# One 8 KB load of a decode kernel taken as five loads of 1, 2, 4, 8 and 113 rows

## The chip, the core and the metric

The kernel runs on one core of a Trainium2 chip. A core has TensorE (PE, matrix multiplies; PEld is its weight load), VectorE (DVE), ScalarE (ACT), GpSimd (POOL) and SyncE (SP, which here only issues transfers), an on-chip memory of 128 partitions (SBUF), an accumulator memory for matmul results (PSUM), and 16 DMA engines that bring data in from HBM. The metric is the device time of one execution in microseconds; less is better.

## What is computed

Two layers, each of attention with a cached K and V (one new token for each of 4 sequences) and a gated feed-forward block, all in float32:

```python
B, Sq, D = 4, 1, 512
Hq, Hkv, Sk, Dh = 32, 8, 4096, 128
def _A_ref(x, k_cache, v_cache, wq, wo):
    q = (x @ wq).reshape(B, Sq, Hq, Dh).transpose(0, 2, 1, 3)
    k = jnp.repeat(k_cache, rep, axis=1)
    v = jnp.repeat(v_cache, rep, axis=1)
    scores = jnp.einsum("bhqd,bhkd->bhqk", q, k) * (Dh ** -0.5)
    p = _softmax(scores, axis=-1)
    o = jnp.einsum("bhqk,bhkd->bhqd", p, v)
    return o.transpose(0, 2, 1, 3).reshape(B, Sq, Hq * Dh) @ wo
def _B_ref(x, w1, w3, w2):          # F = 1792
    h = _silu(x @ w1) * (x @ w3)
    return h @ w2
x = A_x
x = x + _A_ref(_layernorm(x), ...)
x = x + _B_ref(_layernorm(x), ...)
x = x + _A_ref(_layernorm(x), ...)
x = x + _B_ref(_layernorm(x), ...)
```

Both layers use the same caches and weights. K and V together are 128 MB a layer, more than fits on the chip, so most of it is read twice.

## The kernel before

**Data.** The host lays all weights and caches out as one array `rows` of 128 rows; row p is what partition p is to hold. Its columns are counted in units of KB = 256 floats, that is 1 KB a partition and 128 KB over all partitions. In this order stand the projection weights, the caches group by group (a group is one of the 8 KV heads with its 4 query heads, REP = 4), and the feed-forward weights. A group has 32 tiles of 4 units: tiles 0 to 15 are its keys (two chunks of 2048 positions, 8 tiles each), 16 to 31 its values in the same order. In those units the keys of group 1 are 192 to 255 and its values 256 to 319; the keys of group 2 are 320 to 383 and its values 384 to 447, of which the last two tiles are 440 to 447.

**Space and loads.** SBUF holds one tensor `space` of 216 units a partition and, behind them, x. `LOADS` (lines 52 to 66) lists by hand every load in the order in which it is issued, as (first unit in `rows`, units, place in `space`); two entries marked "stash" are copies by ScalarE and no loads. `pump` (line 119) runs when the program is written out: whenever a tile has been used for the last time, `done` (line 148) marks its place free and calls `pump`, which issues as many entries of the list as have their place free, in order, on SP's queue. So a load's place in SP's queue is fixed, and on the chip its issue waits until what was read from its place before has been read. Each load is one `dma_start` at line 139 of all 128 rows (line 136 for the first, which brings x along).

**Compute.** Layer 0 goes through the groups 0 to 7, layer 1 through 7 to 0, so that most of group 7 can stay on the chip from one layer to the next. For each group: `score` (line 322, matmuls at line 333) multiplies q with the keys, `maximum` and `exponent` take the softmax's parts chunk by chunk, `turn` transposes the probabilities, and `weigh` (line 389, matmuls at line 395) multiplies them with the values. The second chunk's weighing stands in `finish`, and DVE adds up its results there (line 416). On PE the order is that of the program: the second weighing of a group stands ahead of the first scores of the next. TensorE takes a tile straight from `space`. Each of these matmuls shows as two in the trace: 32 for a chunk of scores or of weighing, 4 for a tile.

**Around the change,** in layer 1, the list reads (0, 32, 96), (384, 56, 128), (440, 8, 104), (192, 64, 28), (256, 64, 136), (32, 28, 29), (60, 36, 57), (96, 32, 120), and so on to the last values of group 0 and what is left of w3 and w2. (384, 56) are the values of group 2 but for the last two tiles, 7 MB; (440, 8) are those two, 8 KB a row, 1 MB; (192, 64) and (256, 64) are keys and values of group 1, 8 MB each. The keys go to the places 28 to 91. The values go to 136 to 199, on top of values of group 2 from (384, 56), so they wait for most of that group's weighing, but not for its last two tiles. (32, 28), the first keys of group 0, go to 29 to 56, where keys of group 1 lie.

Of the kernel before, what the change touches and what calls it, by code (L numbers as in the profile page):

```python
# [16 lines left out]
P = 128  # L17
# [25 lines left out]
KB = 256  # L43
# [22 lines left out]
)  # L66
BUSY = (4, 1, 2)
SCRATCH = 64

# [5 lines left out]
def tile_decode_layers(ctx: ExitStack, tc: tile.TileContext, rows, out):  # L75
    nc = tc.nc
# [9 lines left out]
    def place(at, n):  # L86
        return space[:, at * KB:(at + n) * KB]
# [31 lines left out]
    def pump():  # L119
        while state["next"] < len(LOADS):  # L120
            src, n, at = LOADS[state["next"]]
            if src == "stash":
                i, n = n, U // KB
                keys = [("kv", TURN, i)]
                if i == 0 and not state["back"]:
                    return
            else:
                keys = [key for key in stream if src <= offset[key] < src + n]
            if any(taken[at:at + n]):
                return  # L130
            taken[at:at + n] = [True] * n
            if src == "stash":
                for j in range(2):
                    nc.scalar.activation(place(at, n)[:, j * BLOCK:(j + 1) * BLOCK], stored[2 * i + j], AF.Copy)
            elif state["next"] == 0:
                nc.sync.dma_start(space[:, at * KB:], rows[:, 0:n * KB + P])
            else:
                lo = src * KB + (P if src else 0)
                nc.sync.dma_start(place(at, n), rows[:, lo:lo + n * KB])
            for key in keys:  # L140
                where[key] = at
                at += size[key[0]]
            state["next"] += 1
# [4 lines left out]
    def done(layer, *key):  # L148
        if layer == 0 and (key[0][:2] == "w1" or key[0] in ("wq", "wo") and key[1] >= HELD or key[:2] == ("kv", TURN) and key[2] in KEPT):
            return  # L150
        at, n = where[key], size[key[0]]
        taken[at:at + n] = [False] * n
        pump()

    pump()


# [47 lines left out]
    def busy(n):  # L205
        if n:
            pt = scores().rearrange("p (k c) -> p k c", k=KC)
            nc.tensor.matmul(pt[:, 0:n, :], ident, ident.unsqueeze(1).to_broadcast([P, n, P]),  # L208
                             start=True, stop=True)

    def small(name, bufs=1):
        return work.tile([P, 1], F32, name=name, tag=name, bufs=bufs)
# [30 lines left out]
    def layernorm(rowsum):  # L243
        xc = deviation(rowsum)
        xT = lay_down(xc)
        ssq = squares(xc)
        rstd = work.tile([P, 2], F32, name="rstd", bufs=1)

        def factor():
            var = o_ps[1][:, 1:2]  # L250
            mean(var, ssq)
            inverse(rstd[:, 0:1], var)

        return xT, rstd, factor
# [170 lines left out]
    def turn_o(o):  # L425
        nc.tensor.matmul(misc[:, 0:B * REP], o, head, start=True, stop=True)  # L426
        nc.vector.tensor_copy(oT[:, :, 0:B], misc[:, 0:B * REP].rearrange("p (b h) -> p h b", b=B))  # L427
# [5 lines left out]
    def project_o(layer, g, rowsum):  # L433
        w = wo_of(g)
        for h in range(REP):
            for k in range(KC):
                nc.tensor.matmul(x_ps[32 * k:32 * k + B, :], oT[:, h, 0:B], w[:, h, k * P:(k + 1) * P],
                                 start=(h == 0), stop=(h == REP - 1))
        done(layer, "wo", g)
        nc.vector.scalar_tensor_tensor(x_sb, x_ps, 1.0, x_sb, op0=ALU.mult, op1=ALU.add,  # L440
                                       accum_out=rowsum)
# [99 lines left out]
    for layer in range(LAYERS):  # L541
# [14 lines left out]
        for n, (g, (first, last)) in enumerate(order):  # L556
# [7 lines left out]
            if layer and n == 0:  # L564
                state["back"] = True
                pump()
# [22 lines left out]
        nc.scalar.activation(spare, half[:, 0:1], AF.Sigmoid)  # L589
        busy(BUSY[0])  # L590
        turn_o(o)
        busy(BUSY[1])
        rowsum = small("rowsum")
        project_o(layer, g, rowsum)
        busy(BUSY[2])
        xT, rstd, factor = layernorm(rowsum)
# [50 lines left out]
```

## Time and profile before

| | us |
|---|---|
| median of 3 runs | 704.23 |
| lowest, highest | 703.98, 705.48 |
| the profiled execution, its own time | 705.11 |
| its span, first to last instruction | 703.2 |
| PE busy in it | 420.1 (60%) |
| DVE busy | 145.8 (21%) |
| mean granted TensorE clock | 0.828 |

The profile shows one execution. Its page gives for each engine the busy time, then the span in 40 equal slices (each digit a share in tenths; here a slice is 17.6 us), the DMA packets and queues, and the chain of work that ended last: from the last instruction back, at each step to what released it. Other views of the same trace are used too: that chain in order of time (start, duration, what), the timeline of instructions (start, duration, engine and line, what is written from what, count, and in brackets the idle time before and what ended it), stretches of time with the busy time of each engine, the granted clock, the DMA engines' share and GB/s, and the DMA issues of a stretch with their size and the time from issue to landing. "SPq" is SP's queue, which issues transfers; "space<-in_rows" is a load.

### The profile page before, as it was taken

To read this page: it belongs to the slowest core of one execution; us is meant where nothing else is said; L and a number is where in the kernel's file an instruction comes from. 1 tells how busy PE (TensorE), PEld (TensorE's weight loads), DVE (VectorE), ACT (ScalarE), POOL (GpSimd) and SP (SyncE) were. 2 spreads that over 40 slices of the span, in tenths; PEclk is the share of its full clock that TensorE was granted. 3 is DMA by queue.
4 is the path that set the end of the run, shared out by engine and by line. 5 is a ranking of instruction groups with operands and counts; after the bars stand their busy time and mean duration, and the time that the engine had idled before them with its cause. 6 is when DMAs were issued, how large, how long until landed. Compare 5 with 4: busy or idle time off the path is not lost.

```text
span 703.2 us, 7344 instructions
## 1 busy us (share of the span) xinstructions
PE 420.1 (60%) x3218; PEld 135.7 (19%) x3218; DVE 145.8 (21%) x508; ACT 41.8 (6%) x100; POOL 3.1 (0%) x10
## 2 busy tenths in 40 slices
PE   1265466644767609767676994734554735557687
PEld 0111121201212103121233331201111201112125
DVE  3012111121121203331221242102120301202232
ACT  0010000000001000000201200100100001000010
POOL 0000000000000000000000000000000000000000
PEclk9997777776698858886998998867977968769899
DMA  9999999999999999999999999999999999999996
GB/s 417 421 418 433 455 418 417 448 440 426 435 427 429 435 429 422 431 431 425 420 403 409 416 433 434 448 425 424 449 430 412 450 418 434 447 426 426 420 419 271
DMA packets 12703, 298.39 MB, mean 424 GB/s; under 512 B 1408, under 2 KB 1536, under 8 KB 4352
## 3 DMA queue, kind: packets, MB, share of 16 engines
q1 hardware_dynamic: 12672, 297.93, 99.0%
q8 instruction: 25, 0.41, 0.2%
q14 instruction: 6, 0.05, 0.0%
HBM read 297.86 MB, written 0.07 MB: 424 GB/s over the span
## 4 chain that ended last, share of the span: by engine, by line
DMA 68%; PE 28%; DVE 2%; another core or an unknown queue 1%; issue 1%; ACT 1%; SPq 0%; ACTq 0%; DVEq 0%
DMA space<-in_rows 68%; PE o L395 10%; PE scores L333 10%; PE turned L359 1%; PE o L469 1%; PE sums_ps L317 1%; PE sums_ps L507 1%; ACT p L352 1%; PE scores L208 1%; PE stored L260 1%; DVE acc L346 1%; PE stored L447 0%; DVE pT L361 0%; PE sums_ps L306 0%
## 5 line engine op out<-in xcount | busy, mean ns | idle before, releaser
L333 PE MATMUL scores<-space,qT 128*32 128x512 f32 x1024 | 172.3, 723 | 145.4 <-DMA space<-in_rows 145.2
L395 PE MATMUL o<-space,pT 128*16 128x512 f32 x1024 | 149.3, 685 | 91.9 <-DMA space<-in_rows 84.8
L333 PEld LDWEIGHTS scores<-space,qT 128*32 128x32 f32 x1024 | 36.4, 125 | 225.6 <-issue 187.8
L395 PEld LDWEIGHTS o<-space,pT 128*16 128x16 f32 x1024 | 32.0, 106 | 187.8 <-issue 94.7
L346 DVE TENSOR_REDUCE acc<-scores 128x1 f32<-128x512 f32 x32 | 22.1, 692 | 185.3 <-PE scores L333 168.2
L352 ACT ACTIVATE p<-scores,acc 128x512 f32<-128x512 f32 x30 | 20.6, 688 | 563.2 <-DVE acc L346 426.7
L416 DVE SCALAR_TENSOR_TENSOR o<-o,acc,o 128x128 f32<-128x128 f32 x112 | 39.3, 351 | 51.0 <-PE o L395 47.6
L361 DVE COPY pT<-turned 128x256 f32<-128x256 f32 x32 | 13.6, 425 | 146.7 <-PE turned L359 146.7
L359 PE MATMUL turned<-ident,p 128*128 128x128 f32 x128 | 22.8, 305 | 12.1 <-ACT p L352 12.1
L306 PE MATMUL sums_ps<-space,xT 128*32 128x512 f32 x120 | 21.7, 718 | 5.9 <-DMA space<-in_rows 5.9
L427 DVE COPY oT<-sums_ps 128x16 f32<-128x16 f32 x16 | 2.8, 175 | 102.6 <-PE sums_ps L426 102.6
L359 PEld LDWEIGHTS turned<-ident,p 128*128 128x128 f32 x128 | 14.6, 150 | 44.1 <-ACT p L352 25.1
L317 PEld LDWEIGHTS sums_ps<-same,shares 128*128 128x128 f32 x120 | 17.1, 220 | 16.9 <-DVE shares L312 11.1
L317 PE MATMUL sums_ps<-same,shares 128*128 128x4 f32 x120 | 18.4, 277 | 1.0 <-DVE shares L312 1.0
L469 PE MATMUL o<-space,xT 128*32 128x192 f32 (+1 forms) x256 | 14.0, 356 | 5.0 <-DVE h L484 2.3
L447 PE MATMUL stored<-space,oT 128*32 128x512 f32 x104 | 13.5, 592 | 0.0
L312 DVE TENSOR_SCALAR shares<-sums_ps,rstd 128x512 f32<-128x512 f32 x15 | 11.1, 743 | 1.8 <-PE sums_ps L306 1.8
L507 PE MATMUL sums_ps<-space,hT 128*4 128x128 f32 x224 | 8.1, 272 | 3.7 <-DMA space<-in_rows 3.2
L216 PE MATMUL o<-rowsum,same 128*128 128x1 f32 x8 | 1.9, 301 | 13.5 <-DVE rowsum L547 13.5
L426 PEld LDWEIGHTS sums_ps<-head,o 128*128 128x128 f32 x32 | 5.9, 232 | 20.1 <-issue 12.5
L469 PEld LDWEIGHTS o<-space,xT 128*32 128x32 f32 x256 | 7.4, 109 | 9.6 <-DVE h L484 3.3
L426 PE MATMUL sums_ps<-head,o 128*128 128x16 f32 x32 | 7.5, 313 | 0.6 <-DVE o L416 0.6
(102 smaller groups left out, 139.3 us busy)
## 6 DMA issues: line engine op xcount, KB each, us to landing
space<-in_rows SPq DMA_DIRECT2D x10, 4096.0 KB, 23.8
space<-in_rows SPq DMA_DIRECT2D x4, 5120.0 KB, 25.8
space<-in_rows SPq DMA_DIRECT2D x14, 1024.0 KB, 13.0
space<-in_rows SPq DMA_DIRECT2D x2, 6144.0 KB, 31.8
space<-in_rows SPq DMA_DIRECT2D x3, 3584.0 KB, 18.6
space<-in_rows SPq DMA_DIRECT2D x2, 4608.0 KB, 19.8
space<-in_rows SPq DMA_DIRECT2D x4, 2048.0 KB, 24.6
space<-in_rows SPq DMA_DIRECT2D x1, 7680.0 KB, 48.8
```

What stands on the lines that cost most here:

```text
L306: nc.tensor.matmul(wide[32 * k:32 * k + 32, :], xT[:, 32 * k:32 * k + 32], w[:, k, :], start=True, stop=True)
L317: nc.tensor.matmul(misc[:, h * B:(h + 1) * B], shares[:, h * DH:(h + 1) * DH], same[:, 0:B], start=True, stop=True)
L333: nc.tensor.matmul(ps[32 * b:32 * b + 32, :], qT[:, b, at:at + 32], t[:, i * BLOCK:(i + 1) * BLOCK], start=(m < 2), stop=(m >= TILES - 2))
L346: nc.vector.tensor_reduce(acc[:, i:i + 1], ps, axis=AX.X, op=ALU.max, negate=True)
L352: nc.scalar.activation(p.rearrange("p n s -> p (n s)"), ps, AF.Exp, bias=acc[:, i:i + 1], scale=1.0 if scale is None else scale, accum_out ...
L359: nc.tensor.transpose(pt[:, n, :], p[:, n, :], ident)
L361: nc.vector.tensor_copy(pT, pt.rearrange("p n (b r) -> p n b r", b=B)[:, :, :, 0:ROW])
L395: nc.tensor.matmul(o_ps[i][32 * b:32 * b + ROW, :], pT[:, r // 2, b, :], t[:, j * NB * DH:(j + 1) * NB * DH], start=(r < 2), stop=(r >= TI ...
L416: nc.vector.scalar_tensor_tensor(o, o_ps[s][:, j * DH:(j + 1) * DH], acc[:, 16 + NB * s + j:17 + NB * s + j], o, op0=ALU.mult, op1=ALU.add)
L447: nc.tensor.matmul(bank[32 * h:32 * h + 32, :], oT[:, h, :], w[:, h, :], start=first, stop=last)
L469: nc.tensor.matmul(bank[32 * j:32 * j + 32, s], xT[:, 32 * k:32 * k + 32], w[:, j], start=(k == 0), stop=(k == KC - 1))
L507: nc.tensor.matmul(x_ps[32 * k:32 * k + B, :], hT[:, m, :], t[:, k * P:(k + 1) * P], start=False, stop=(m == 13))
```

## The change

Two constants are added, and the load that begins at unit 440 of `rows`, and it alone, is issued as five: rows 0, 1 to 2, 3 to 6, 7 to 14 and 15 to 127, that is 1, 2, 4, 8 and 113 rows. Each brings 8 KB a row into the same place as before, and all stand where the one stood in SP's queue.

```diff
+BY_ROWS = 440
+ROWS = 0, 1, 3, 7, 15, P
...
             else:
                 lo = src * KB + (P if src else 0)
-                nc.sync.dma_start(place(at, n), rows[:, lo:lo + n * KB])
+                for a, b in zip(ROWS, ROWS[1:]) if src == BY_ROWS else ((0, P),):
+                    nc.sync.dma_start(place(at, n)[a:b], rows[a:b, lo:lo + n * KB])
```

The bytes loaded, their places and all arithmetic stay as they are. The matmuls of the last two value tiles of group 2 now depend on five loads.

## The prediction

> **What bounds the kernel now.** I read the page first, its slices and its counts of DMA packets.
>
> ```profile
> span 703.2 us, 7344 instructions
> DMA  9999999999999999999999999999999999999996
> DMA packets 12703, 298.39 MB, mean 424 GB/s; under 512 B 1408, under 2 KB 1536, under 8 KB 4352
> q1 hardware_dynamic: 12672, 297.93, 99.0%
> DMA 68%; PE 28%; DVE 2%; another core or an unknown queue 1%; issue 1%; ACT 1%; SPq 0%; ACTq 0%; DVEq 0%
> ```
>
> The 16 DMA engines are busy in every slice but the last, so what sets the end is how many bytes each of them has to carry. The counts tell how a load is shared out. The program has 88 transfers (87 loads and the store). 1408 packets under 512 B are 88 x 16: a small piece on every engine for every transfer. The loads' queue holds 12672 = 88 x (128 + 16) packets: each row is one packet. So every load of 128 rows is dealt out as 8 rows an engine, and all engines stay level.
>
> Then the chain of waits in order of time, around the changed load (X, the last two value tiles of group 2) and at the end.
>
> ```profile
> 558.42 42.40 DMA space<-in_rows
> 600.86 5.29 PE o L395 x32
> ...
> 607.25 2.81 PE o L395 x24
> 610.08 32.29 DMA space<-in_rows
> 642.41 4.99 PE o L395 x32
> ...
> 656.44 26.10 DMA space<-in_rows
> 682.58 1.06 PE o L395 x4
> ...
> 700.56 0.29 DVE space L599
> ```
>
> The first piece is the 7 MB load ahead of X; it lands at 600.8. The weighing at 607.25 has 32 matmuls; after 24 of them the chain jumps to an issue at 610.08. Those 24 use the 7 MB load, the last 8 use X. So V, the value load of group 1, is issued before X is touched. From the last landing at 682.5 there follow 20.7 us of arithmetic.
>
> The SP queue and the landings of X, of K (keys of group 1) and of V, each from the view of issues in a stretch of a microsecond or less; the last columns are KB (left out for 8 MB) and us to landing.
>
> ```profile
> 585.91 6.21 SPq L139 DMA_DIRECT2D space<-in_rows  x2
> space<-in_rows SPq DMA_DIRECT2D x1, 1024.0 KB, 17.4
> 591.79 66.02 SPq L139 DMA_DIRECT2D space<-in_rows  x11
> space<-in_rows SPq DMA_DIRECT2D x1, 30.8
> 610.08 0.33 SPq L139 DMA_DIRECT2D space<-in_rows  x1
> space<-in_rows SPq DMA_DIRECT2D x1, 32.3
> ```
>
> X is issued at 585.91 and lands at 603.3, K at 591.79 and 622.6, V at 610.08 and 642.4. X waits 15 us behind older work: the queue is never empty here.
>
> **The change part by part.** First, what one row costs an engine. Columns of these stretches: the engines' busy times and counts, clock, DMA share, GB/s.
>
> ```profile
> 390.00:400.00 10.00, 8.80 (x76) 3.14 (x72) 2.44 (x5) 2.93 (x6) 0.00 (x0) 1.00 1.03 425
> 603.30:622.60 19.30, 7.06 (x60) 1.75 (x52) 4.43 (x17) 0.00 (x0) 0.00 (x0) 0.77 1.00 431
> 690.00:696.00 6.00, 5.39 (x114) 3.34 (x106) 1.17 (x2) 0.64 (x1) 0.35 (x1) 1.00 0.97 394
> 696.00:698.00 2.00, 1.72 (x35) 1.05 (x37) 0.72 (x4) 0.00 (x0) 0.00 (x0) 1.00 0.55 219
> 698.00:700.00 2.00, 2.00 (x84) 1.96 (x77) 0.20 (x2) 0.00 (x0) 0.00 (x0) 1.00 0.12 38
> ```
>
> In the first stretch the rows are of 8 KB, as X's: 425 / 16 = 26.6 GB/s an engine, so 8192 B take 0.308 us. An engine does not get faster when others stop: at 690 to 696 a busy engine moves 394 / (16 x 0.97) = 25.4 GB/s, at 696 to 698, with half of them idle, 219 / (16 x 0.55) = 24.9.
>
> *Removed:* one load, 8 rows an engine, 8 x 0.308 = 2.5 us.
>
> *Added: loads of 1, 2, 4 and 8 rows.* Bounds: nothing saved or lost if they are spread, one row each (1.2 us in all) on whichever engine gets a row of every one. With whole rows in equal shares, 2, 4 and 8 rows go one to an engine; I put about 3 rows, 0.9 us, on the engine that also gets the big piece.
>
> *Added: one load of 113 rows.* No transfer of before has a row count that 16 doesn't divide, so the price is bounded from both sides. If rows are dealt out unevenly, engines get 7 or 8: no cost. In equal shares of whole rows, which is all that the packet counts show, 113, a prime, can only go to one engine (or be 113 shares): 113 x 0.308 = 34.8 us there. I take equal shares, the only pattern that the counts bear out. The loaded engine then has 116 rows in place of 8: 108 x 0.308 = 33.3 us more, and nothing takes rows off it afterwards, since all later loads again give it its 8. The DMA slices show no idle time to catch up in.
>
> [...]
>
> *What the others do meanwhile.* They finish X's few rows at once and fill the same 128 partitions with K and V, both already issued, until about 642. The loaded engine writes into partitions that they are writing into as well. Its rows begin at 600.8 + 0.9 = 601.7. Bounds: undisturbed, the last is down at 601.7 + 34.8 = 636.5, 33.2 us after X's 603.3. If it gets nothing next to others and only its own sixteenth (7 rows) goes through, 106 rows remain at 642: 642 + 32.6 = 674.6, or 71.3 us. Each stream keeps its rate however many others run, so the limit sits with the engine or with its way into the memory, not in a common pool; if with the way in, two streams that meet there get half each. I take half: 0.616 us a row, (642 - 601.7) / 0.616 = 65 rows by 642, 4 of them in its own sixteenth and so 1.2 us cheaper, and 48 x 0.308 = 14.8 us for the rest: 655.6, which is 52.3 us late.
>
> [...]
>
> *Where the stall goes.* PE waits from 610 for X until about 656 and has 8 matmuls left. Behind it on PE stand the scores of group 1, which now start with K:
>
> ```profile
> 622.77 3.64 PE L333 MATMUL scores<-space,qT 128*32 128x512 f32 x16 [11.90 <-DMA space<-in_rows]
> ```
>
> K's rows on the loaded engine follow X's and take 19.3 us: 655.6 + 19.3 = 674.9 for 622.6, late by the same 52.3. So the wait for X isn't added to this. V follows 19 us later. The next load after V goes where K lies, so its issue waits for those scores and moves along; the loaded engine still has V to carry then and never runs dry. All that follows keeps its distances; the fifteen other engines idle once, for as long as the loaded one is behind.
>
> *Four more issues* on SP, 0.33 us each, end by 588, ahead of K's issue at 591.79. The matmuls that read X wait for up to five completions in place of one: some tens of ns on a PE that stands idle. Both cost nothing; with no cover, under 2 us.
>
> *The engine's place.* At the end the engines run dry one after another, from 696 to 700 (shares 0.97, 0.55, 0.12). The end of before follows the last of them. The loaded one may be that or up to 4 us ahead; I take 2 us off.
>
> *Sum:* 52.3 - 2 = 50.3 us on the span of 703.2: 753.5. The profiled execution took 705.11, 0.9 more than the median of 704.23, so against the median: **754.5 us.**
>
> **The rivals.** *One engine, undisturbed:* 33.2 - 2 = 31.2, so 735.4; 733.4 to 737.5 by the engine's place. For it: nothing in the trace shows one engine slowing another; the limit may be in the engine itself. *One engine, held back:* its rows go through only when others pause: 71.3 - 2, so 773.5. Against it: sixteen streams run side by side at share 1.00 with none starved. *Rows dealt out over all engines* (or the load cut again on its way to the chip), 7 or 8 rows each: not slower. The place is the dealing out of the 113 rows, the price four issues that the backlog of 15 us covers, and it decides as long as no engine gets over about 4 rows more than 8 (4 x 0.308 = 1.2 us, under 0.2%): 704.2. Against it: the even counts. A load that is simply late but harmless is ruled out: K stands behind it on the same engine.
>
> **How the numbers follow.** About half a share: 0.54, with a range of its own from 745 to 763. One engine, undisturbed: 0.25. Held back further: 0.09. Dealt out: 0.08. Something else, such as a share of the rows on a few engines: 0.04. The range from 733 to 763 holds the first two, and leaves out most of the rest, just under 2 in 10. About 0.2% (1.4 us) can be told from no change. Slower: 0.91; within: 0.07, nearly all from the dealing out; faster: 0.02, if the order of small pieces happens to relieve the last engine.
>
> **What would show it.** The DMA slices: 9 until about 642, then 0 or 1 (one engine of sixteen) while that engine works off its rows, until the load after V is issued, which in before came 7.7 us after K's landing (next row): to about 682 by the forecast, 664 if undisturbed; then 9 again, since all carry the same rows from there on.
>
> ```profile
> 630.32 0.33 SPq L139 DMA_DIRECT2D space<-in_rows  x1
> ```
>
> The rest: X's 113 rows landing near 655 for the forecast, near 637 if undisturbed, near 675 if held back; PE idle after 24 of 32 matmuls at 610. Small packets: with 113 rows on one engine the changed load has one completion piece for them, with all 16 engines it has 16. Wrong at once: DMA slices that stay at 9 throughout, or X landing before 606.

## The result, and the profile after

| | before | after |
|---|---|---|
| median, us | 704.24 (703.98 to 705.48) | 758.56 (757.66 to 761.42) |
| the profiled execution: its time, its span | 705.11, 703.2 | 761.42, 759.6 |

Taking this 1 MB load (8 KB a row) as five makes the kernel slower: ratio 1.0774, 95% interval 1.0758 to 1.079, that is 54.3 us by the medians. The forecast was 50.3 us, 754.5. The profiled execution of after is the slowest of its five, 2.9 us over their median.

The page of after, its span, DMA slices (19 us each), rate, packets and loads' queue:

```profile
span 759.6 us, 7351 instructions
DMA  9999999999999999999999999999999979208993
GB/s 390 442 439 439 438 406 449 424 432 432 440 414 449 413 434 430 434 424 406 410 394 418 431 448 435 415 449 432 415 446 434 396 280 350 104 28 352 427 380 135
DMA packets 12703, 298.39 MB, mean 393 GB/s; under 512 B 1408, under 2 KB 1536, under 8 KB 4352
q1 hardware_dynamic: 12672, 297.93, 93.1%
```

The same bytes in the same number of packets, but two slices at 2 and 0 tenths, with 104 and 28 GB/s, and ahead of them one at 7, with 280. 28 GB/s is about one engine's rate (425 / 16 = 26.6 in before). The packet counts are those of before to the last piece: one load of 128 rows made 128 + 16 packets, and five loads make the same sum only if their completion pieces number 16 together. Equal shares give 1 + 2 + 4 + 8 + 1. With the slices of one engine's rate this says that the 113 rows ran on one engine.

The chain in order of time, the lines that answer to those of before:

```profile
558.72 44.64 DMA space<-in_rows
603.41 5.61 PE o L398 x32
...
610.12 2.77 PE o L398 x24
612.89 47.16 issue
660.04 1.91 PE o L398 x8
661.95 17.22 another core or an unknown queue
679.17 0.14 issue
679.31 3.50 PE scores L336 x16
...
698.58 5.80 PE o L398 x32
...
713.42 24.21 DMA space<-in_rows
737.68 1.06 PE o L398 x4
...
742.49 13.07 DMA space<-in_rows
755.60 0.62 PE sums_ps L510 x16
```

PE stops after 24 of 32 matmuls, as forecast, and stands for 47 us ("issue" and "unknown queue": the view couldn't tie the wait to a load's landing there). X is usable at 660.0, K at 679.3, V at 698.6, where before had 603.3, 622.8 and 642.4: late by 56.7, 56.5 and 56.2. From K on everything keeps its distance. The last value load is 55.1 late (737.68 for 682.58), so 1.6 us came back; and the tail is 1.3 us longer (759.6 - 737.68 = 21.9 for 20.6), since at the end the chain now runs through the last weights' loads as well.

Stretches of after (the columns as in the prediction) and the packets of one of them:

```profile
626.00:628.00 2.00, 0.00 (x0) 0.00 (x0) 0.00 (x0) 0.00 (x0) 0.00 (x0) 0.50 0.07 29
630.00:650.00 20.00, 0.00 (x0) 0.00 (x0) 0.00 (x0) 0.00 (x0) 0.00 (x0) 0.50 0.97 351
654.00:659.00 5.00, 0.00 (x0) 0.00 (x0) 0.00 (x0) 0.00 (x0) 0.00 (x0) 0.50 0.06 26
661.00:679.00 18.00, 0.95 (x8) 0.00 (x0) 1.40 (x4) 0.00 (x0) 0.00 (x0) 0.50 0.07 29
```

```profile
DMA packets 136, 7.02 MB, mean 351 GB/s; under 512 B 0, under 2 KB 0, under 8 KB 0
```

From 654 a share of 0.06, one engine of sixteen, at 26 GB/s. It is the same from 626 to 628, between K and V. The packets are those of 630 to 650, when all engines ran; they are of 8 KB (X's rows) and 64 KB (V's) alone, so two equations give both counts: 33 and 103 (33 x 8192 + 103 x 65536 = 7.02 million). 33 rows in 20 us are 0.606 us a row, where the forecast had 0.616 for half a share. The records of single packets show more. All 113 of the loaded engine are there, end to end from 601.76 to 659.38. Counted from row 15, rows 29 to 40 are these (start in us, ns):

```
row 29  610.04 426   row 30  610.45 713   row 31  611.14 720   row 32  611.85 658
row 33  612.50 315   row 34  612.81 312   row 35  613.12 312   row 36  613.43 319
row 37  613.75 408   row 38  614.14 729   row 39  614.85 705   row 40  615.54 668
```

Rows 33 to 36 go at full speed with the other engines at work (share 0.90, 355 GB/s from 612.5 to 613.7); the groups of four around them cost 2.5 us in place of 1.25. No run here tells why these four were spared, or why the pattern goes by fours.

### The profile page after: what moved, and what is told of

It is laid out like the page before. It is cut to its first block, busy times and chain, and to the rows that moved or that the text cites. A ratio compares the mean times of both kernels' runs of the same rounds, so it can differ in the third digit from the quotient of the medians.

```text
span 759.6 us, 7351 instructions
## 1 busy us (share of the span) xinstructions
PE 425.9 (56%) x3218; PEld 135.5 (18%) x3218; DVE 145.7 (19%) x508; ACT 41.7 (5%) x100; POOL 3.1 (0%) x10
## 2 busy tenths in 40 slices
DMA packets 12703, 298.39 MB, mean 393 GB/s; under 512 B 1408, under 2 KB 1536, under 8 KB 4352
## 4 chain that ended last, share of the span: by engine, by line
DMA 61%; PE 25%; issue 7%; another core or an unknown queue 4%; DVE 2%; ACT 0%; SPq 0%; ACTq 0%; DVEq 0%
DMA space<-in_rows 61%; PE o L398 11%; PE scores L336 9%; PE turned L362 1%; PE sums_ps L320 1%; DVE pT L364 1%; PE stored L263 0%; ACT p L355 0%; DVE o L419 0%; PE sums_ps L309 0%; DVE acc L349 0%; PE stored L450 0%; PE sums_ps L510 0%; PE o L472 0%
## 5 line engine op out<-in xcount | busy, mean ns | idle before, releaser
L336 PE MATMUL scores<-space,qT 128*32 128x512 f32 x1024 | 174.3, 729 | 149.9 <-DMA space<-in_rows 149.6
L398 PE MATMUL o<-space,pT 128*16 128x512 f32 x1024 | 152.4, 702 | 138.4 <-DMA space<-in_rows 84.5
L355 ACT ACTIVATE p<-scores,acc 128x512 f32<-128x512 f32 x30 | 20.6, 687 | 618.5 <-DVE acc L349 485.3
L472 PE MATMUL o<-space,xT 128*32 128x192 f32 (+1 forms) x256 | 15.6, 379 | 4.2 <-DVE h L487 2.3
## 6 DMA issues: line engine op xcount, KB each, us to landing
space<-in_rows SPq DMA_DIRECT2D x4, 2048.0 KB, 19.3
```

Of the source, the lines that this page charges most:

```text
L336: nc.tensor.matmul(ps[32 * b:32 * b + 32, :], qT[:, b, at:at + 32], t[:, i * BLOCK:(i + 1) * BLOCK], start=(m < 2), stop=(m >= TILES - 2))
L355: nc.scalar.activation(p.rearrange("p n s -> p (n s)"), ps, AF.Exp, bias=acc[:, i:i + 1], scale=1.0 if scale is None else scale, accum_out ...
L398: nc.tensor.matmul(o_ps[i][32 * b:32 * b + ROW, :], pT[:, r // 2, b, :], t[:, j * NB * DH:(j + 1) * NB * DH], start=(r < 2), stop=(r >= TI ...
L472: nc.tensor.matmul(bank[32 * j:32 * j + 32, s], xT[:, 32 * k:32 * k + 32], w[:, j], start=(k == 0), stop=(k == KC - 1))
```

## The experiments

In each, one thing differs from the change or from before. "Late" is against the 704.1 to 704.2 of before, measured beside them.

**The 113 rows cut once more.**

```diff
-ROWS = 0, 1, 3, 7, 15, P
+ROWS = 0, 1, 3, 7, 15, 127, P
```

> The load's last part of 113 rows is cut once more, into 112 and 1: six loads of 1, 2, 4, 8, 112 and 1 rows. Theory (equal shares of whole rows, 113 on one engine): 112 = 16 x 7 is dealt over all engines, nobody has more than about 11 rows in place of 8, under 1 us: 704 to 705.5, the time of before. Rival (the number of loads, of completions or of issues costs): one more load than the change has, so 758 or more.

Measured: 710.07, ratio 1.0076 (1.0059 to 1.0093). One row is moved out of the last load, and 48 us of the 54 are gone; the rival is out. But 6.0 us remain where the theory had at most 1.4. The stretch in which X lands, before and here:

```profile
598.00:606.00 8.00, 5.14 (x32) 0.99 (x32) 0.00 (x0) 0.00 (x0) 0.00 (x0) 0.61 1.06 456
```

```profile
598.00:606.00 8.00, 0.56 (x4) 0.15 (x8) 0.00 (x0) 0.00 (x0) 0.00 (x0) 0.50 1.11 261
```

All engines are busy (1.06 and 1.11), at 456 and at 261 GB/s. Nobody has too many rows; the rows go slowly.

**The small loads as one of 15 rows.**

```diff
-ROWS = 0, 1, 3, 7, 15, P
+ROWS = 0, 15, P
```

> The four small loads are taken as one of 15 rows; 113 rows stay one load. Theory: the loaded engine has 114 rows in place of 116, 2 x 0.62 = 1.2 us less than the change: 756 to 759. Rival (the small loads or the count of five cost a good part of the 54 us): well under 750.

Measured: 756.63, ratio 1.0741 (1.0725 to 1.0757). 1.9 us below the change, so the rival is out: neither the small loads nor the number of loads makes the 54 us. That the 1.2 us of the forecast came out so nearly is in part luck, since more than the row count differs. SP's issue of K took 20.0 us here (last section), so rows 19 to 57 of the 113 passed at 0.31 us before K was there, and the other engines stood nearly idle meanwhile (share 0.06 from 602 to 611); the later rows then ran beside K and V. The records count 73 slow rows, for 78 in the change.

**Two loads of 10 and 118 rows.**

```diff
-ROWS = 0, 1, 3, 7, 15, P
+ROWS = 0, 10, P
```

> Two loads of 10 and 118 rows; 118 = 2 x 59. Theory (the largest number of equal shares up to 16, half speed beside the others): 59 rows on each of two engines and one of the ten, 60 x 0.62 = 37 us from 601, so X lands at 638 and the keys behind it at 658, 35 us late: 735 to 742. If rows cost 0.308 us there (no sharing): 16 us late, 718 to 722. If every count that 16 does not divide goes to one engine: 758 to 762.

Measured: 734.52, ratio 1.0431 (1.0413 to 1.0449), half a microsecond under the range given and far from both rivals.

From its page, a stretch, and the chain:

```profile
DMA packets 12699, 298.39 MB, mean 407 GB/s; under 512 B 1404, under 2 KB 1532, under 8 KB 4348
```

```profile
604.00:622.00 18.00, 8.56 (x60) 1.97 (x52) 3.03 (x13) 0.00 (x0) 0.00 (x0) 0.78 1.01 259
```

```profile
634.82 1.91 PE o L398 x8
636.73 17.04 another core or an unknown queue
653.91 3.64 PE scores L336 x16
```

1404 = 1408 - 16 + 12: ten completion pieces for 10 rows and two for 118. X comes at 634.8, 31.5 us late: 59 rows a loaded engine, nearly all beside other traffic.

**The change with a wait added.** SP stores 512 bytes of the changed load's last row ahead of K's issue, so K and V start only when the 113 rows are down.

```diff
+                if src == 192 and state["next"] > 60:
+                    nc.sync.dma_start(out[P - 1:P], loaded("kv", 2, 30)[P - 1:P, 0:P])
```

> The change, with a wait added: ahead of the issue of the keys of group 1, SP issues a small store of 512 bytes from the last row of the changed load to the output (overwritten at the end), so keys and values are issued only when the 113 rows are down, and no other engine moves data beside them. Theory (rows are slow because other engines fill the same partitions): 113 x 0.312 = 35.3 us from 601.7, X lands at 637, the keys start some 2 us later and land near 659, 36 us late in place of 56: 736 to 743, some 18 us faster than the change although a wait was added. Rival (113 rows on one engine cost 0.5 us each by themselves): X lands at 660 as in the change, and the wait comes on top: 760 to 764.

Measured: 739.06, ratio 1.0491 (1.0475 to 1.0506): 19.5 us faster than the change, with a wait more. The timeline at the end of X (SP's store, then the matmuls that use X), and the packets between 603 and 634:

```profile
634.83 0.24 SPq L142 DMA_DIRECT2D out<-space  x1
634.98 0.18 PEld L400 LDWEIGHTS o<-space,pT 128*16 128x16 f32 x8 [24.89 <-issue]
635.01 1.91 PE L400 MATMUL o<-space,pT 128*16 128x512 f32 x8 [23.99 <-issue]
```

```profile
DMA packets 100, 0.82 MB, mean 26 GB/s; under 512 B 0, under 2 KB 0, under 8 KB 0
q1 hardware_dynamic: 100, 0.82, 6.3%
```

100 rows in 31 us, 0.310 us each, on one engine (6.3% of sixteen). X is down at 634.8 in place of 660.0; 2.8 of these 25 us come from rows that began earlier (599.0 for 601.8). The same 113 rows, again on one engine, to the same places: what made them slow was the traffic beside them. What the wait itself costs was measured on before:

> Before, with the same added store of 512 bytes ahead of the keys of group 1 and so the same wait for the load, which is whole here. It tells what the wait costs by itself: the engines stand idle from 603.3 until the keys start some 2 us later: 706 to 708.

Measured: 708.89, ratio 1.0067 (1.0052 to 1.0082): 4.8 us, more than the 2 to 4 expected.

```profile
603.50:605.30 1.80, 1.80 (x16) 0.39 (x12) 0.00 (x0) 0.00 (x0) 0.00 (x0) 0.72 0.00 0
```

The engines move nothing for 1.8 us after X's landing; the rest isn't resolved. One candidate is that those engines that were ahead of the last one lose that lead at the wait.

**The same split on a load near the end.** The load of before is whole, and the one from unit 1216 in layer 1 is split.

```diff
-BY_ROWS = 440
+BY_ROWS = 1216
...
-                for a, b in zip(ROWS, ROWS[1:]) if src == BY_ROWS else ((0, P),):
+                for a, b in zip(ROWS, ROWS[1:]) if (src, n) == (BY_ROWS, 8) else ((0, P),):
```

> The load of before is left whole, and another of the same size near the end (from unit 1216 in layer 1, landing near 696 in before) is taken as 1, 2, 4, 8 and 113 rows. Only 12 KB a row come behind it, so the other engines run dry about 5 us later. Theory: nearly all rows go at 0.312 us: 108 x 0.312 = 33.7 us, up to 3 us more for sharing at first, up to 4 less by the engine's place: 733 to 740. Rival (the rows are slow by themselves, 0.5 us each): 108 x 0.5 = 54 us: 755 or more.

Measured: 737.69, ratio 1.0474 (1.0456 to 1.0491), 33.6 us late. The same rows cost 20 us less where little else is on the way; the records count 11 slow rows of 113, for 78 in the change:

```profile
710.00:728.00 18.00, 0.00 (x0) 0.00 (x0) 0.00 (x0) 0.00 (x0) 0.00 (x0) 0.50 0.11 40
```

**8 and 120 rows.**

```diff
-ROWS = 0, 1, 3, 7, 15, P
+ROWS = 0, 8, P
```

> Two loads of 8 and 120 rows; 120 = 15 x 8. Theory: 8 rows on each of 15 engines, and one each of the 8 rows: nobody has more than 9 rows, 0.3 us: 704 to 705. If every count that 16 does not divide goes to one engine: 758 to 764.

Measured: 709.48, ratio 1.0077 (1.0062 to 1.0092). Not one engine, and its page has 1415 small packets = 1408 - 16 + 8 + 15: 120 rows go over 15 engines.

```profile
DMA packets 12710, 298.39 MB, mean 422 GB/s; under 512 B 1415, under 2 KB 1543, under 8 KB 4359
```

But again 5.4 us where next to nothing was expected. What the even splits share isn't a high count of rows on one engine. A supposition: a row of a smaller load goes to another engine than in a load of 128, and there it meets the engine that fills its partition in the loads around. The rival is the number of loads; two runs tell the two apart.

**By columns, and in halves.**

```diff
-                nc.sync.dma_start(place(at, n), rows[:, lo:lo + n * KB])
+                for i, j in ((0, 1), (1, 2), (2, 4), (4, 6), (6, 8)) if src == 440 else ((0, n),):
+                    nc.sync.dma_start(place(at + i, j - i), rows[:, lo + i * KB:lo + j * KB])
```

> The load is taken as five again, but cut by columns: each has all 128 rows, of 1, 1, 2, 2 and 2 KB. Theory (rows that come to another engine than usual meet that engine's stream and go at half speed): here every row stays with its engine, five smaller packets a row cost some tens of ns more, 0.3 us for 8 rows: 704 to 705. Rival (five or six loads in place of one cost the 5 to 6 us that 112 + 1 and 8 + 120 rows were over before): 708 to 711.

```diff
-ROWS = 0, 1, 3, 7, 15, P
+ROWS = 0, 64, P
```

> The load is taken as two of 64 rows, 4 rows an engine in each, so 8 rows an engine in all. Theory: the counts are even, but half or more of the rows come to another engine than the one that fills their partitions in the loads around: 3 to 6 us, 707 to 710. Rival (an even deal over 16 engines is free): 704 to 705.

Measured: five loads by columns 705.13, ratio 1.0006 (0.9994 to 1.0018), no difference that can be told. Two halves by rows 709.78, ratio 1.0065 (1.0045 to 1.0084), 5.6 us. Their stretches, columns first:

```profile
598.00:606.00 8.00, 4.80 (x24) 0.97 (x28) 0.00 (x0) 0.00 (x0) 0.00 (x0) 0.51 1.16 473
```

```profile
598.00:606.00 8.00, 1.90 (x12) 0.49 (x16) 0.00 (x0) 0.00 (x0) 0.00 (x0) 0.50 1.03 231
```

Five loads by columns are free; two loads of equal halves by rows are not. So the 5 to 6 us don't come from the number of loads but from the cut by rows. The records show the rows slow: on the mean 0.59 us each in the halves, 0.59 with 112 and 1 and 0.57 with 8 and 120, for 0.31 in before. That they meet another engine's stream fits this; it isn't shown, since the records don't tell which engine carried a row.

## Why the prediction was right, step by step

**Right: what bounds the kernel, and the shares.** The time followed the rows on the most loaded engine: 758.56 with 113 rows of one load on one engine, 734.52 with 59, 710.07 with 7. Equal shares of whole rows, over the largest number of engines up to 16 that divides the count, gave each count of small packets that was measured: 112 on 16 engines (1424), 120 on 15 (1415), 118 on 2 (1404), 113 on 1 (1408). The page of the profile with 112 rows:

```profile
DMA packets 12719, 298.39 MB, mean 421 GB/s; under 512 B 1424, under 2 KB 1552, under 8 KB 4368
```

1424 = 1408 - 16 + 1 + 2 + 4 + 8 + 16 + 1.

**Right: the price of a row alone.** 0.308 us forecast, 0.310 in the run with the wait.

**Right: half speed beside others.** 0.616 forecast, 0.606 measured in after; the run with the wait, at 0.310, shows that the traffic beside the rows is the cause. The half was a choice between two bounds, so that it came out so well is in part luck. The rival of an undisturbed engine (735.4) is what came out where the others were kept away: 739.1 with the wait, which by itself costs 4.8, and 737.7 near the end. The range of 733 to 763 held that rival too; the half's own range, 745 to 763, leaves it out and holds the 758.56. That the streams meet on the way into the on-chip memory was the author's supposition; no run shows where they meet.

**Mis-sized: how long the others run beside it.** "Until about 642", said the prediction, so 65 rows beside them, 4 of these at full speed, and 48 alone. In after the others were done near 652.7. They lost speed: 351 GB/s at a share of 0.97, against 431 at 1.00 before, where the sum had left out any slowing of them. And V's issue, which took 0.33 us before, held SP for 14.8:

```profile
612.95 14.83 SPq L142 DMA_DIRECT2D space<-in_rows  x1
```

K was down on the fifteen others by 626.0 and V came to them at 628.4. Between, and again from 652.7, they had nothing to do, where the prediction had them idle once. The records count 78 slow rows (0.61 us on the mean) and 35 fast ones, where the sum has 61 and 52. 17 rows at 0.3 us are about the 4.4 us by which X came later than forecast (660.0 for 655.6).

**Small: the engine's place.** 2 us off in the forecast; 1.6 came back between X and the last value load, and 1.3 went at the end, where the chain now runs through the last weights' loads: 0.3 in all.

**Right: where the stall goes.** The wait for X wasn't added to K's; K, V and the end are late by nearly the same. The four issues and the five completions cost nothing that shows: K's issue came at 591.25, for 591.79 in before, and five loads by columns took 705.13.

**Too cheap: rows dealt out evenly.** The rival of 704.2 took an even deal to cost nothing. Where the rows were dealt out nearly or wholly evenly (112 and 1, 8 and 120, 64 and 64), 5.4 to 6.0 us were measured: a cut by rows has a price of its own.

Not tried: two streams meeting in one partition range with the number of engines otherwise equal, which would tell the way into those partitions from other shared ways into the memory or out of HBM.

## What to carry to other kernels

In a kernel bound by DMA, count the rows on the most loaded engine, not the bytes: cut a load by columns, all 128 rows each time (0.1% here, not to be told from nothing), and not by rows (5 to 6 us even where the counts are even, 54 us where a prime count puts 113 rows on one engine). A lagging engine also pays for its neighbours' haste: holding back the next loads until it was through made the changed kernel 19.5 us faster. Before blaming the number of transfers, read the packet counts: they tell over how many engines each was dealt (1404 small ones with 118 rows on two engines, 1415 with 120 on fifteen).

## What the runs showed of the hardware that was not expected

- *One intruding stream slows all.* In the 20 us from 630 to 650 of after, X's 33 rows would alone have taken 33 x 0.308 = 10 us of one engine's time, but fifteen engines moved 103 packets of 64 KB where the 19.3 us for 8 rows of before would have let them move 124 (15 x 20 / 2.41): 21 packets, 51 us of engine time. With two intruders (10 and 118 rows) the rate fell to 259 GB/s at a share of 1.01. Why more is lost than the intruders bring is open.
- *An issue can hold SP for 15 to 20 us* when one engine has many packets ahead. With 15 and 113 rows it was K's issue:

```profile
591.11 19.99 SPq L142 DMA_DIRECT2D space<-in_rows  x1
```

  By the records, both holds ended when 72 to 74 rows were left for that engine; with 59 rows each on two engines, V's issue took 0.35 us. That a limit on what may be queued for one engine holds SP is a guess from these three. The loaded engine had work all along; the others ran out, from 626 to 628 in after and from 602 to 611 with 15 and 113 rows.
